# Fewer preparing steps, earlier hash products and later loads in batch one of a hash-attention and SwiGLU kernel

## The chip, the cores and the metric

The kernel runs on one core of one Trainium2 chip. The metric is device time in microseconds (us), measured on the chip; every run's output was compared with the reference and was correct unless said otherwise. A run counts as fast when it is within 1.5% of the fastest of its kernel.

## The reference, cut to what matters

```python
def _attn_ref(q, k, v, proj):              # q, k, v: 4 x 8 x 768 x 64, proj: 64 x 6
    q_bits = (einsum('bhsd,dk->bhsk', q, proj) > 0)
    k_bits = (einsum('bhsd,dk->bhsk', k, proj) > 0)
    mask = q_bucket[:, :, :, None] == k_bucket[:, :, None, :]    # buckets from the 6 bits
    scores = np.where(mask, scale * q @ k.T, -1e9)
    attn = softmax(scores)
    return attn @ v
def _moe_ref(x, w_gate, w_val, w_out):     # x: 3072 x 512, d_ff 1536
    g = x @ w_gate
    return (g * sigmoid(g) * (x @ w_val)) @ w_out
```

The attention's output (4 batches of 768 rows, 8 heads of 64) is x, reshaped to 3072 x 512.

## The kernel before

Two heads make a pair; each batch has four pairs, and each pair is worked in two halves of 384 queries with six score units each. While batch one's attention runs there is no expert product to fill gaps with, so its halves follow each other on TensorE: six score units, then six attend products. The hash products of a pair (L403) are turned into signs by ScalarE, and a transfer on the SP queue (the sign transfer, L420) copies those of q to a second place, where the score products read them. In between, VectorE prepares the expert weights for later in small steps: three per weight piece (L302, L304, L307) and four for the block sums of a finished group (L336), after which GpSimd writes the blocks to DRAM and fetches the first ones back.

The main loop, cut:

```python
for u in range(0, N, NCH):                 # u: first score unit of a half, NCH = 6
    n, half, _ = units[u]
    gating = u >= LATE                     # true once batch one's attention is over
    for c in range(NCH):
        score(u + c)
        if u + c == 2 or not gating and half == 1 and c == NCH - 3:
            prepare_pair(1)                # hash products of the next pair
        if c == 1 and half == 0 and 0 < n <= NP:
            total(n - 1)                   # softmax sums of the pair before
        if c:
            add(u + c)                     # VectorE, L514 and L518
    if n <= NP:
        finish(waiting)                    # norm of the pair before, L551
        finish(rest)
    ...
    for c in range(NCH):
        attend(u + c)
    if half == 1:
        load(n + 2, "qkv" if gating else "v")
    elif not gating:
        prepare_pair(2 if u > 0 else 4)
        load(n + 2, "qk")
    finish(first)
    prepare_on(0 if u == LATE else 4)      # preparing steps
    ...
    prepare_on(0 if LATE - NCH <= u <= LATE else 3)
```

The softmax sums and their reciprocal. The sum uses the one `av` buffer of PSUM that the attend products use too, and the reciprocal is spread over the partitions by eight 48 KB transfers on the SP queue:

```python
def total(n):
    ps = av_ps.tile([P, 512], FP32, tag="av", name="sum") if b == 0 else bank("sum")
    for h in range(2):
        for half in range(2):              # L531
            nc.tensor.matmul(ps[g : g + BLOCK, 0:HQ], ones, t[half][:, h, :], ...)
    nc.vector.reciprocal(r, ps[:, 0:HQ])   # L539
    for half in range(2):
        for h in range(2):
            for at in (h * D, h * D + BLOCK):
                nc.sync.dma_start(t[at : at + BLOCK, half, :], r[g : g + BLOCK, :])   # L544
    waiting.append(lambda: norm(n, t))     # norm is L551, on VectorE
```

Of the kernel before, what the change touches and what calls it, by code (L numbers as in the profile page):

```python
# [18 lines left out]
def kernel(  # L19
# [16 lines left out]
    NCH = S // P  # L36
# [3 lines left out]
    NP = H // 2  # L40
# [36 lines left out]
    def fetch(n, name, queue, half=None):  # L77
        b, pr = pairs[n]
        if name == "v":
            t = raws["v", n] = raw.tile([P, 2, NCH, D], FP32, tag="vraw", name="vraw")  # L80
            queue.dma_start(
                t.rearrange("p h c d -> p h (c d)"),
                v[b, 2 * pr : 2 * pr + 2].rearrange("h (p c) d -> p h (c d)", c=NCH),
            )
            return
        src = q if name == "q" else k
        if not half:
            raws[name, n] = raw.tile([P, NCH, 2, D], FP32, tag=name + "raw", name=name + "raw",
                                     bufs=1)
        t = raws[name, n]  # L90
        if n <= NP:
            cs = slice(None) if half is None else slice(half * CH, (half + 1) * CH)
            for h in range(2):
                queue.dma_start(t[:, cs, h, :],
                                src[b, 2 * pr + h].rearrange("(p c) d -> p c d", c=NCH)[:, cs, :])
            return


        blocks = t.rearrange("p c a b -> p (c a b)").rearrange(
            "p (c a d) -> p c a d", a=P // BLOCK, d=BLOCK)  # L100
        for h in range(2):
            for x in range(D // BLOCK):
                at = h * D + x * BLOCK
                queue.dma_start(  # L104
                    blocks[at : at + BLOCK],
                    src[b, 2 * pr + h][:, x * BLOCK : (x + 1) * BLOCK].rearrange(
                        "(a p c) d -> p c a d", c=NCH, p=BLOCK))

    def load(n, names):
        if n < len(pairs):  # L110
            for name in names:
                fetch(n, name, nc.sync)
# [179 lines left out]
    def scale_ahead():  # L292
        scale_to(min(progress["piece"] + 4, progress["scaled"] + 1))
# [70 lines left out]
    def prepare_on(n):  # L364
        for _ in range(n):
            next(preparing, None)
# [102 lines left out]
    LATE = NP * 2 * NCH  # L469
# [5 lines left out]
    def score(u):  # L475
        n, half, c = units[u]
        qs = slice(half * HQ, (half + 1) * HQ)
        ks = slice(c * P, (c + 1) * P)
        sc = [bank("sc")[:, 0:HQ] for _ in range(2)]
        for x, start in ((T, True), (bits, False)):  # L480
            if u < 2 and not start:
                prepare_pair(1)
            for h in range(2):
                rows = slice(h * D, (h + 1) * D)
                nc.tensor.matmul(sc[h], x["k", n][rows, ks], x["q", n][rows, qs],  # L485
                                 start=start, stop=not start)
        for h in range(2):
            nc.scalar.activation(weights(u)[:, h, 0:HQ], sc[h], AF.Exp,  # L488
                                 scale=SCALE * (OFF / 2 if n <= NP else 1.0))
# [19 lines left out]
    def add(u):  # L509
        n, half, c = units[u]  # L510
        a = weights(u)
        if c == 1:
            acc[n, half] = att.tile([P, 2, HQ], FP32, tag="acc", name="acc")
            nc.vector.scalar_tensor_tensor(out=acc[n, half], in0=weights(u - 1)[:, :, 0:HQ],  # L514
                                           scalar=S * EPS / P, in1=a[:, :, 0:HQ],
                                           op0=ALU.add, op1=ALU.add)
        elif c > 1:
            nc.vector.tensor_tensor(acc[n, half], acc[n, half], a[:, :, 0:HQ], op=ALU.add)  # L518

    def total(n):  # L520



        b, pr = pairs[n]

        ps = av_ps.tile([P, 512], FP32, tag="av", name="sum") if b == 0 else bank("sum")
        t = [acc.pop((n, half)) for half in range(2)]
        for h in range(2):
            for half in range(2):
                g = (2 * h + half) * BLOCK  # L530
                nc.tensor.matmul(ps[g : g + BLOCK, 0:HQ], ones, t[half][:, h, :],  # L531
                                 start=True, stop=True)
        if b == 0:
            space = wo.rearrange("p f m -> p (f m)")
            space = space[:, n % 2 * 3 * HQ : (n % 2 + 1) * 3 * HQ].rearrange("p (x q) -> p x q", q=HQ)
            r, t = space[:, 2, :], space[:, 0:2, :]
        else:
            r, t = t[1][:, 0, :], t[0]
# [3 lines that stand above are left out]
                g = (2 * h + half) * BLOCK  # L542
                for at in (h * D, h * D + BLOCK):
                    nc.sync.dma_start(t[at : at + BLOCK, half, :], r[g : g + BLOCK, :])  # L544
        waiting.append(lambda: norm(n, t))
        if pr == NP - 1:
            push_ffn(b)
# [200 lines left out]
    def prepare_pair(count):  # L748
        for _ in range(count):
            rest.extend(f for f in steps.pop(0)() or [] if f)  # L750

    def finish(todo):
        while todo:
            todo.pop(0)()
# [5 lines left out]
    for u in range(0, N, NCH):  # L760
        n, half, _ = units[u]
        gating = u >= LATE
        if u == MOVE:
            progress["late"] = True
            for t in late_ring:
                nc.gpsimd.memset(t[:, :, HQ:AW], 1.0)
        for c in range(NCH):
            score(u + c)
            if u + c == 2 or not gating and half == 1 and c == NCH - 3:
                prepare_pair(1)  # L770
            if c == 1 and half == 0 and 0 < n <= NP:
                total(n - 1)
            if c:
                add(u + c)
        if n <= NP:
            finish(waiting)
            finish(rest)
        if not gating and half == 0:
            steps = front(n + 1)
        if not gating and half == 0 and u > 0:  # L780
            prepare_pair(2)
        for _ in range(1 if u else 2):
            scale_ahead()
        for c in range(NCH):
            attend(u + c)
        if not gating:
            scale_ahead()
        if half == 1:
            load(n + 2, "qkv" if gating else "v")
        elif not gating:  # L790
            prepare_pair(2 if u > 0 else 4)
            load(n + 2, "qk")
        finish(first)
        prepare_on(0 if u == LATE else 4)
        chores = []
        if half == 1 and n >= NP:
            total(n)
            if n + 1 < len(pairs):
                chores = [None] + steps.pop(0)()
        prepare_on(0 if LATE - NCH <= u <= LATE else 3)  # L800
        if not gating:
            continue
        if n + 1 < len(pairs) and half == 0:
            steps = front(n + 1)
            chores = [None, steps.pop(0), None, steps.pop(0)]

        credit += 14 if n < 2 * NP else 15.75
        end = True
        part = 0
        while atoms and (credit > 0 or not end):  # L810
            size, atom, end = atoms.pop(0)
            credit -= size
            atom()
            part += size
            if part >= 11 or u + NCH == N and part >= 6:
                finish(waiting)
                if u + NCH == N:
                    finish([first.pop(0) for _ in range(min(2, len(first)))])
            if 5 < part < 14 if u == LATE else part < 9:
                prepare_on(size)  # L820
            if 6 < part < 11 or u == LATE and part > 10:
                scale_ahead()
            for _ in range(size):
                if chores:
                    step = chores.pop(0)
                    chores.extend(step and step() or [])
        while chores:
            step = chores.pop(0)
            chores.extend(step and step() or [])
# [34 lines left out]
```

## Time and profile before

| | |
|---|---|
| median of the first 3 runs | 1002.44 us (1001.71 to 1003.04) |
| TensorE busy | 990.2 of 1000.3 us in the profiled run |
| first expert product (L575) | 113.72 us |
| waits of TensorE in batch one of 0.3 us and more | 1.67 and 1.38 (reciprocal), 0.35 (additions), 1.17 (signs) |

How to read the views: an instruction's row in order of time is start, duration, engine, source line, operation, what it writes and reads, how many were run together, and in brackets how long its engine had been idle before it and what ended that. SPq and POOL rows of DMA operations are issues; the time to landing is told apart. Two more rows of the kernel before will matter. The first is from VectorE in order of time, the second from the list of DMA issues (count, size of each, median us from issue to landing):

```profile
93.74 1.02 DVE L551 SCALAR_TENSOR_TENSOR xT<-xT,e,wo 128x768 f32<-128x768 f32 x1 [1.46 <-DMA wo<-wo]
```

```profile
wo<-wo SPq DMA_DIRECT2D x32, 48.0 KB, 2.7
```

VectorE waits 1.46 us for the spread reciprocal of the fourth pair's half before it can go on with its queue, and the 32 transfers that spread batch one's reciprocals take 2.7 us in the median.

### The profile page before, as it was taken

The numbers are of one execution on the slowest core, as the hardware profiler recorded it, in microseconds if no ns is written. First come the engines' busy times: TensorE is split into PE (matmuls) and PEld (weight loads), VectorE is DVE, ScalarE is ACT, GpSimd is POOL, SyncE is SP. The second block draws the span as 40 slices with busy tenths as digits, with TensorE's granted clock in tenths as the row PEclk, the third lists the DMA queues.
The fourth block names the chain that finished last, engine by engine and source line by source line (L and its number), as shares of the span: only waits on it lengthen the run. The fifth ranks groups of instructions, "written<-read, shape, count | busy, mean of one in ns | idle before, by whom it ended". The sixth has DMA issues, their size and how long they took to land.

```text
span 1000.3 us, 12465 instructions
## 1 busy us (share of the span) xinstructions
PE 990.2 (99%) x4597; PEld 599.8 (60%) x4597; DVE 570.7 (57%) x892; ACT 398.4 (40%) x885; POOL 101.5 (10%) x200
## 2 busy tenths in 40 slices
PE   9999999999999999999999999999999999999998
PEld 4444455555576765555557775555556786555687
DVE  5888998887873624556564443554556442435431
ACT  6988555465323214444342223334343211222200
POOL 3222022221000000000000000000000000111000
PEclk9999999999999999999999999999999999999999
DMA  7777595885213032333331204333122012323001
GB/s 230 214 252 244 146 259 161 216 291 148 76 43 76 22 96 84 87 100 95 97 103 34 69 17 116 92 90 100 44 84 77 22 38 64 105 82 111 29 27 37
DMA packets 120749, 106.95 MB, mean 107 GB/s; under 512 B 89264, under 2 KB 104080, under 8 KB 120688
## 3 DMA queue, kind: packets, MB, share of 16 engines
q0 software_dynamic: 19104, 73.28, 22.9%
q1 hardware_dynamic: 100784, 32.67, 14.3%
q8 instruction: 36, 0.59, 0.3%
q10 hardware_dynamic: 800, 0.20, 0.1%
q14 instruction: 25, 0.20, 0.1%
HBM read 81.79 MB, written 17.30 MB: 99 GB/s over the span
## 4 chain that ended last, share of the span: by engine, by line
PE 87%; DMA 2%; DVE 1%; SPq 1%; ACT 1%; issue 1%; POOL 0%; DVEq 0%; POOLq 0%
PE up L575 43%; PE po L575 22%; PE sc L485 12%; PE av L500 9%; PE sum L531 1%; DMA words<-in_moe_w_out_dram 1%; PE hps L403 1%; SPq L104 1%; DMA wo<-wo 1%; DMA qb<-qb 0%; DMA room<-ram 0%; DVE room L359 0%; ACT A L488 0%; DVE wo L539 0%; DVE acc L518 0%
## 5 line engine op out<-in xcount | busy, mean ns | idle before, releaser
L575 PE MATMUL up<-xT,room 128*128 128x384 f32 x768 | 260.9, 488 | 0.0
L575 PEld LDWEIGHTS up<-xT,room 128*128 128x128 f32 x768 | 144.6, 190 | 106.7 <-issue 9.8
L575 PE MATMUL up<-xc,room 128*128 128x384 f32 x576 | 197.4, 486 | 0.0
L485 PE MATMUL sc<-qT,kT 64*128 64x384 f32 x768 | 161.5, 494 | 0.2 <-DVE c L562 0.2
L575 PEld LDWEIGHTS up<-xc,room 128*128 128x128 f32 x576 | 109.5, 190 | 76.3
L579 DVE TENSOR_TENSOR c<-c,up 128x384 f32<-128x384 f32 x72 | 39.8, 553 | 180.1 <-PE up L575 179.7
L518 DVE TENSOR_TENSOR acc<-acc,A 128x768 f32<-128x768 f32 x128 | 122.7, 958 | 14.4 <-ACT A L488 1.0
L318 POOL DMA_DIRECT2D room<-ram x96 | 52.4, 546 | 714.3 <-PE up L575 707.2
L488 ACT ACTIVATE A<-sc 128x384 f32<-128x384 f32 x256 | 105.6, 499 | 3.5 <-PE sc L485 3.4
L485 PEld LDWEIGHTS sc<-qT,kT 64*128 64x128 f32 x768 | 67.8, 186 | 55.5 <-issue 45.7
L710 ACT COPY o<-po 128x256 f32<-128x256 f32 x48 | 17.9, 372 | 200.5 <-PE po L575 200.5
L561 ACT ACTIVATE th<-c 128x384 f32<-128x384 f32 x72 | 37.6, 522 | 128.7 <-DVE c L562 89.2
L500 PE MATMUL av<-A,vraw 128*64 128x384 f32 (+1 forms) x512 | 88.2, 486 | 0.0
L579 DVE TENSOR_TENSOR o<-o,po 128x256 f32<-128x256 f32 x36 | 15.2, 421 | 111.6 <-PE po L575 82.5
L485 PE MATMUL sc<-qb,kb 64*128 64x384 bf16 x384 | 65.4, 323 | 1.7 <-DMA qb<-qb 1.2
L488 ACT ACTIVATE room<-sc 128x384 f32<-128x384 f32 x128 | 54.0, 495 | 32.6 <-PE sc L485 32.6
L575 PE MATMUL po<-wo,hid 128*128 128x256 f32 x288 | 66.9, 382 | 0.0
L575 PE MATMUL po<-wo,room 128*128 128x256 f32 x288 | 66.3, 379 | 0.1
L575 PE MATMUL po<-room,hid 128*128 128x256 f32 x288 | 66.1, 379 | 0.0
L500 PEld LDWEIGHTS av<-A,vraw 128*64 128x64 f32 x512 | 36.7, 137 | 46.0 <-issue 44.1
L638 ACT COPY c<-up 128x384 f32<-128x384 f32 x72 | 34.4, 478 | 69.1 <-PE up L575 69.1
L575 PEld LDWEIGHTS po<-wo,hid 128*128 128x128 f32 x288 | 54.1, 190 | 12.1 <-issue 4.9
(110 smaller groups left out, 969.4 us busy)
## 6 DMA issues: line engine op xcount, KB each, us to landing
room<-ram POOLq DMA_DIRECT2D x48, 512.0 KB, 4.8
room<-ram POOLq DMA_DIRECT2D x48, 384.0 KB, 3.9
vraw<-in_v_dram SPq DMA_DIRECT2D x16, 384.0 KB, 3.3
ram<-room POOLq DMA_DIRECT2D x12, 512.0 KB, 4.8
out_dram<-o SPq DMA_DIRECT2D x48, 128.0 KB, 1.7
room<-in_moe_w_out_dram POOLq DMA_DIRECT2D x10, 512.0 KB, 6.3
qraw<-in_q_dram SPq DMA_DIRECT2D x48, 96.0 KB, 3.2
hid<-in_moe_w_gate_dram POOLq DMA_DIRECT2D x9, 512.0 KB, 6.9
```

The lines of the kernel that those rows point to most:

```text
L104: queue.dma_start(blocks[at : at + BLOCK], src[b, 2 * pr + h][:, x * BLOCK : (x + 1) * BLOCK].rearrange("(a p c) d -> p c a d", c=NCH, p=B ...
L318: nc.gpsimd.dma_start(places[k % 2][:, PARTS[go], :], ram[k % NG][:, PARTS[go], :])
L403: nc.tensor.matmul(tile_[i * BLOCK : (i + 1) * BLOCK, 0:HQ], hash_w, T[name, n][:, half * HQ : (half + 1) * HQ], start=True, stop=True)
L485: nc.tensor.matmul(sc[h], x["k", n][rows, ks], x["q", n][rows, qs], start=start, stop=not start)
L488: nc.scalar.activation(weights(u)[:, h, 0:HQ], sc[h], AF.Exp, scale=SCALE * (OFF / 2 if n <= NP else 1.0))
L500: nc.tensor.matmul(ps[h * D : (h + 1) * D, 0:width], raws["v", n][:, h, c, :], a[:, h, 0:width], start=c == 0, stop=c == NCH - 1)
L518: nc.vector.tensor_tensor(acc[n, half], acc[n, half], a[:, :, 0:HQ], op=ALU.add)
L561: nc.scalar.activation(th, g, AF.Tanh, scale=0.5)
L575: nc.tensor.matmul(ps, a, x, start=start and i == 0, stop=i == len(pairs_) - 1, skip_group_check=True)
L579: nc.vector.tensor_tensor(o, a, b, op=op)
L638: nc.scalar.copy(tile_of(g, spot), c)
L710: nc.scalar.copy(o, c)
```

## The change

The intent is to take the three kinds of stall in batch one away. (A) VectorE has two preparing steps fewer after each second half of batch one, so that additions and reciprocal come earlier; the steps are caught up in batch two. (B) The hash products come one score unit earlier in second halves. (C) The sixth pair's q and k loads move from the fourth pair's first half to the end of its second half, behind the transfer of signs that waited for them on the SP queue.

```diff
-            if u + c == 2 or not gating and half == 1 and c == NCH - 3:
+            if u + c == 2 or not gating and half == 1 and c == 2:
                 prepare_pair(1)
...
         if half == 1:
-            load(n + 2, "qkv" if gating else "v")
+            load(n + 2, "qkv" if n + 2 > NP else "v")
         elif not gating:
             prepare_pair(2 if u > 0 else 4)
-            load(n + 2, "qk")
+            if n + 2 <= NP:
+                load(n + 2, "qk")
...
-        prepare_on(0 if LATE - NCH <= u <= LATE else 3)
+        prepare_on(0 if LATE - NCH <= u <= LATE else 3 if gating or not half else 1)
...
-            if 5 < part < 14 if u == LATE else part < 9:
+            if 5 < part < 14 if u == LATE else part < (9 if u < LATE + 3 * NCH else 11):
                 prepare_on(size)
```

## The prediction

> **What bounds the kernel now.** I read the page's first part first, then busy time by stretch, then the order-of-time lists of TensorE, VectorE and the SP queue, and last the chain of waits.
>
> ```profile
> PE 990.2 (99%) x4597; PEld 599.8 (60%) x4597; DVE 570.7 (57%) x892; ACT 398.4 (40%) x885; POOL 101.5 (10%) x200
> ```
>
> TensorE is busy for 99% of the span, and the change neither adds nor removes a matmul. So only TensorE's stalls can be won, and they are few. Busy time by stretch, cut at the borders of the score-and-attend halves of batch one, shows where:
>
> ```profile
> 43.41:53.45 10.04, 10.04 (x69) 4.42 (x68) 7.45 (x11) 9.91 (x22) 2.43 (x5) 1.00 0.60 156
> 53.45:67.63 14.18, 12.46 (x82) 5.83 (x80) 13.32 (x16) 10.25 (x25) 4.80 (x8) 1.00 0.94 344
> 67.63:77.68 10.05, 10.05 (x69) 4.42 (x68) 7.42 (x12) 9.92 (x22) 0.58 (x1) 1.00 0.58 154
> 77.68:92.12 14.44, 12.65 (x83) 5.84 (x81) 13.68 (x16) 10.34 (x25) 3.71 (x7) 1.00 0.85 292
> ```
>
> The columns are: stretch, its length, then busy time of PE, PEld, DVE, ACT and POOL. Second halves (10.04, 10.05) have no stall. A first half adds a sum (0.78) and two sets of transposes (0.80 each), so some 11.45 us would do. The third and fourth pairs' first halves take 14.18 and 14.44: 2.7 and 3.0 us lost, with DVE busy for 94% of them. TensorE in order of time names the stalls:
>
> ```profile
> 60.25 0.87 PE L387 MATMUL tps<-ident,kraw 128*128 128x128 f32 x6
> 62.79 1.52 PE L500 MATMUL av<-room,vraw 128*64 128x386 f32 x8 [1.67 <-DVE wo L539]
> ...
> 87.27 1.52 PE L500 MATMUL av<-room,vraw 128*64 128x386 f32 x8 [1.38 <-DVE wo L539]
> ...
> 104.41 0.32 PE L485 MATMUL sc<-qb,kb 64*128 64x384 bf16 x1 [1.17 <-DMA qb<-qb]
> ```
>
> The attend product waits for the reciprocal (L539) because both use the one av buffer of PSUM. A stretched sum adds to it (the sum at 55.39 took 1.49 where 0.85 is usual). VectorE just before that reciprocal:
>
> ```profile
> 55.90 0.69 DVE L307 CUSTOM_DVE_ANT_0 room<-hid,room 128x1024 uint16<-128x1024 uint16 x1
> 56.50 0.42 DVE L302 TENSOR_SCALAR room<-room 128x512 int32<-128x512 int32 x1
> 56.96 0.69 DVE L304 SCALAR_TENSOR_TENSOR room<-hid,room 128x512 int32<-128x512 int32 x1
> 57.68 0.69 DVE L307 CUSTOM_DVE_ANT_0 room<-hid,room 128x1024 uint16<-128x1024 uint16 x1
> 58.29 0.42 DVE L302 TENSOR_SCALAR room<-room 128x512 int32<-128x512 int32 x1
> 58.75 0.69 DVE L304 SCALAR_TENSOR_TENSOR room<-hid,room 128x512 int32<-128x512 int32 x1
> 59.57 0.69 DVE L307 CUSTOM_DVE_ANT_0 room<-hid,room 128x1024 uint16<-128x1024 uint16 x1
> 60.18 2.55 DVE L539 RECIPROCAL wo<-sum 128x384 f32<-128x384 f32 x1
> ```
>
> Seven preparing steps of the expert weights, 4.3 us, stand between the last addition and the reciprocal. The third stall, at 104.41, is the SP queue's: the sign transfer's wait for the queue.
>
> ```profile
> 92.46 2.75 SPq L104 DMA_DIRECT2D qraw<-in_q_dram  x4
> 95.25 3.83 SPq L104 DMA_DIRECT2D kraw<-in_k_dram  x4
> 99.59 0.55 SPq L420 DMA_DIRECT2D qb<-qb  x1
> ```
>
> The signs were ready on ScalarE at 97.9; the transfer was issued at 99.59 behind eight loads, and landed 4.8 us later.
>
> **What the Trainium skill says.** "PSUM — Partial Sum Buffer", section "Engine vs sequencer instructions": the queues of ScalarE, VectorE and GpSimdE are strict FIFO. The trace agrees: the reciprocal at 60.18 starts when the seventh step is over, though its sum was complete at 56.8. "DMA: Bandwidth & Descriptors", section "Anatomy of one DMA": a transfer has a fixed part of about 2 us, mostly the receipt of the last byte. The sign transfer's median of 1.9 us agrees; the one of 4.8 was among the loads. "Perfetto Trace Analysis", section "Identifying Performance Opportunities" (Optimization Strategy), says to find the gaps of the engine in question and what it waits for; that is the method here.
>
> **The change part by part.**
>
> 1. *Two steps fewer.* The order of instructions shows, between the last addition of a second half and the next reciprocal, 5 steps instead of 7 in front of the second, third and fourth pairs (4 of the fifth pair in both). All 144 steps remain; the missing 6 are made up by 2 more in each of three later halves (batch two's fourth to sixth). I walked VectorE by durations (L302 0.34 to 0.46, L304 0.72, L307 0.61, L336 0.67, reciprocal 2.46 to its successor, the five accumulations 5.05, L551 0.93).
>  - Second pair: the two L336 leave (1.34), the reciprocal is earlier, but TensorE never waited there.
>  - Third pair: the additions of the half before end at 54.95 instead of 55.9, so the sum isn't stretched (0.65); five steps (3.0) and the reciprocal end at 60.45. TensorE's transposes end at 60.75, so the stall goes: attend at 60.75 instead of 62.79, **2.0 us won**.
>  - Fourth pair: reciprocal end 60.45, plus 7.4 until the spread reciprocal is back (as in the trace), L551, seven steps (4.4), five accumulations: 78.15. Five steps (2.8) and the reciprocal: 83.45. Attend at 83.5 instead of 87.27, **3.8 won in all**.
>  - Fifth pair: 83.45 plus 6.6, L551, 4.3 of steps, 5.05: 100.3; L307 and three L336 (2.65) and the reciprocal: 105.4. Attend at 105.45 instead of 109.68: **4.2 in all**. VectorE is then the limit, and TensorE waits about 0.9 again. L551 behind it costs the first expert products about 0.2, so **4.0** is left.
> 2. *Loads behind the sign transfer.* That stall (1.2) goes, but it lies within the 4.2 above: without part 1's earlier additions the next limit is VectorE anyway. The loads move to about 94 us; their reader is VectorE's transpose at 120 (now some 116), so they hide.
> 3. *Hash products one unit earlier.* TensorE's and ScalarE's work is the same. The signs of q come 0.8 us earlier, useful only for the transfer. But the product's PSUM buffer (seven in turn) comes round one score unit earlier, at the first unit of the next half, and is read by the last sign of k, which ended 0.1 to 0.25 us after that unit's start (31.71 against 31.50; 53.56 against 53.45). That costs 0.1 to 0.3 in two places; the first is counted above (attend 0.16 later in the second pair), the second too.
> 4. *The bill in batch two.* The catching-up steps end where the expert products already stall: 1.07, 0.92 and 0.4 us at the starts of the halves at 216.8, 245.2 and 274.9. The chain of waits shows the first:
>
> ```profile
> 208.16 0.45 POOL room L318
> 208.61 0.07 issue
> 208.68 7.47 DMA words<-in_moe_w_out_dram
> 216.15 0.02 issue
> 216.18 0.67 ACT wo L288
> ```
>
>  A load of a weight piece stands behind a fetch of blocks in GpSimd's queue; ScalarE stops for it, then the gating, then a PSUM buffer. In the changed order another piece takes that place: it also has to wait for the copies of the last block, about 6 us later than now, so I put it 0 to 1 us later. In the second half the last waiting load stands behind the second fetch instead of the first (1.3 us): 0 to 1 later. In the third, two more L359 (0.6 each) fall into VectorE's unbroken run before 279: 0.3 to 1.2. I take 0.5, 0.5 and 0.7: **1.7 us lost**.
>
> Sum: 4.0 less 1.7 is 2.3 us; 1002.44 less 2.3 is about 1000.1.
>
> **The rivals.**
> - *The new bound is VectorE throughout batch one, so the gain is smaller.* For: its chain from reciprocal to reciprocal (23 us then 22) is as long as TensorE's work there, and the SP queue's eight spreads took 5.0 to 5.9 us. With 7.4 instead of 6.6 at the two later places it loses 1.6: a time of 1001.7. Against: the two later ones did take 6.5.
> - *The late stalls grow more.* For: pieces are two later all through the first expert halves, and loads took up to 9.4 us there. At 2 us for each of the first two, all is paid back: 1002 to 1003. Against: the catching up is done before the weights' last use, and the pieces in question are loaded at much the same places.
> - *Late stalls vanish, since fewer steps crowd them.* Then all 4 us stay: 998.4. For: three of the four waiting loads come earlier in that half. Against: the fourth does not.
> - *The hash move stalls more than said, or ScalarE becomes the limit* (it is busy 9.9 of 10.05 in second halves). Up to 0.3 at each of four places: 1001.
>
> **Range and chances.** The gain in batch one is 3 to 4.3, the loss later 0 to 3.5; with the spread of the runs before (1001.71 to 1003.04) I say 1000.1, and 998.4 to 1002.0 for 8 in 10. All visible stalls add to some 10 us, half of what 2% asks for (20 us), so faster by 2% can't come from this; slower by 2% would need a stall seen nowhere here. Chances: 0.005, 0.99, 0.005.
>
> **What would show it right or wrong.** Right: the wait for L539 before attends gone in the third pair, under 0.7 in the fourth, about 1 in the fifth; no wait for the sign transfer; a first score unit of a second or third pair held by 0.1 to 0.3; the first expert product near 109.5 instead of 113.7; late stalls at the three halves of 1 to 2 us each. Wrong: that product later than 111 (VectorE or the spreads bound it), or less than 1 us of the lead left after 330 us (the late stalls grew), or 4 us of it (they didn't).

## More of the kernel before

What a preparing step can set off on GpSimd's queue:

```python
def form(n):
    ...                                    # two block writes from the stage (L328, L330)
    for o, x, y, op in (...):
        nc.vector.tensor_tensor(o, x, y, op=op)      # L336
        yield True
    for pair, i in enumerate(group):
        nc.gpsimd.dma_start(ram[i][:, S2 : S4 + 1, :], formed[:, pair, :, :])   # L339
        if i < 2:
            for go in range(2):
                bring(i, go)               # L318: fetch of a block back from DRAM
# narrow(i) ends with load_words(i): L273, loads of the next weight pieces, 512 KB each
```

## The result and the profile after

The changed kernel takes **1007.97 us** in the median of 4 runs (1006.93 to 1008.95); the kernel before took 1002.08 (1000.92 to 1003.04) in its 4 runs. The ratio is **1.0059** (95% interval 1.0042 to 1.0077). Ratios here are the mean time of one kernel's fast runs over that of the other's fast runs of the same rounds, so they are not quite the ratio of the medians. The time is 7.9 us above the predicted 1000.1 and outside the predicted range. The change made the kernel about 6 us slower. All outputs are right.

The same part of the page, and busy time by stretch of the kernel after (stretch, length, busy PE, PEld, DVE, ACT, POOL, granted clock with 1.00 for full speed, DMA share, GB/s), cut at the third, fourth and fifth pairs' first halves:

```profile
PE 994.0 (99%) x4597; PEld 601.1 (60%) x4597; DVE 570.1 (57%) x892; ACT 399.9 (40%) x885; POOL 101.2 (10%) x200
```

```profile
53.95:67.13 13.18, 12.44 (x80) 5.64 (x78) 12.45 (x14) 10.19 (x24) 3.42 (x7) 1.00 0.91 317
77.20:91.16 13.96, 12.60 (x84) 5.85 (x82) 13.16 (x15) 10.14 (x24) 3.23 (x6) 1.00 0.61 190
101.18:137.17 35.99, 31.40 (x126) 15.86 (x125) 32.21 (x49) 16.42 (x35) 7.61 (x13) 0.91 0.61 157
```

The fifth pair's first half, which includes the first expert products, in the kernel before:

```profile
102.20:132.01 29.81, 28.64 (x128) 15.02 (x126) 27.18 (x42) 16.47 (x36) 3.53 (x7) 1.00 0.60 159
```

The first stretch is cut 0.19 us late: the third pair's first score product stands at 53.76. From first score product to first score product that half got 0.80 us shorter (14.18 to 13.38) and the fourth's 0.50 (14.44 to 13.94). The fifth's got 6.18 us longer: idle time of TensorE grew from 1.17 to 4.59 us (3.42 more), and its busy time from 28.64 to 31.40 (2.76 more) for the same work, at a mean granted clock of 0.91. TensorE in order of time shows both:

```profile
62.30 1.52 PE L500 MATMUL av<-room,vraw 128*64 128x386 f32 x8 [0.24 <-DVE wo L539]
...
81.09 0.85 PE L531 MATMUL sum<-acc,ones 128*32 128x384 f32 x6 [1.25 <-DVE acc L518]
...
86.29 1.52 PE L500 MATMUL av<-room,vraw 128*64 128x386 f32 x8
...
108.42 1.50 PE L531 MATMUL sum<-acc,ones 128*32 128x384 f32 x6 [4.59 <-DVE acc L518]
109.85 1.65 PE L485 MATMUL sc<-qT,kT 64*128 64x384 f32 x4
...
118.91 8.01 PE L575 MATMUL up<-xT,room 128*128 128x384 f32 x24
```

The waits for the reciprocal (L539) are nearly gone, and so is the wait for the signs, as intended. In their place TensorE waits 4.59 us for the additions (L518) of the fourth pair, before the sum at 108.42. After that wait a group of four score products takes 1.65 us where 0.92 is usual; between 107 and 113 us the granted clock is 0.50. The attends of the third and fourth pairs come 0.5 and 1.0 us earlier than before; the first expert product comes 5.2 us later (118.91 against 113.72).

Why the additions are late is on VectorE, in order of time:

```profile
83.68 2.55 DVE L539 RECIPROCAL wo<-sum 128x384 f32<-128x384 f32 x1
...
87.15 4.15 DVE L518 TENSOR_TENSOR acc<-acc,A 128x768 f32<-128x768 f32 x4
98.05 1.02 DVE L551 SCALAR_TENSOR_TENSOR xT<-xT,e,wo 128x768 f32<-128x768 f32 x1 [6.75 <-DMA wo<-wo]
...
103.16 0.95 DVE L514 SCALAR_TENSOR_TENSOR acc<-room 128x768 f32<-128x768 f32 x1
```

The reciprocal starts 1.0 us earlier than before (83.68 against 84.67). But L551, which needs the spread, stands next in the queue and waits **6.75 us** instead of 1.46. All behind it waits too: seven preparing steps and the additions of the second half, which begin at 103.16 instead of 99.11.

The spread took so long because of what ran beside it. Issues of GpSimd in order of time, the kernel before first, then the kernel after:

```profile
78.26 1.09 POOL L318 DMA_DIRECT2D room<-ram  x2 [3.55 <-issue]
...
79.87 0.53 POOL L273 DMA_DIRECT2D words<-in_moe_w_val_dram  x1
80.39 0.53 POOL L273 DMA_DIRECT2D hid<-in_moe_w_val_dram  x1
```

```profile
85.40 1.09 POOL L318 DMA_DIRECT2D room<-ram  x2 [2.89 <-issue]
86.48 0.54 POOL L339 DMA_DIRECT2D ram<-room  x1
87.01 0.53 POOL L273 DMA_DIRECT2D words<-in_moe_w_val_dram  x1
87.53 0.53 POOL L273 DMA_DIRECT2D hid<-in_moe_w_val_dram  x1
```

The eight issues of the spread on the SP queue, before and after:

```profile
87.24 5.04 SPq L544 DMA_DIRECT2D wo<-wo  x8
```

```profile
86.26 6.32 SPq L544 DMA_DIRECT2D wo<-wo  x8
```

On GpSimd's queue it is the same burst of about 2.4 MB by the sizes in the list of DMA issues: two fetches of blocks (512 and 384 KB), a write of blocks and two loads of weight pieces (512 KB each). It follows the last L336 step. That step ended at about 73.8 us in the kernel before and at about 81.6 in the kernel after, since two fewer steps in each second half pushed it from one pair's half into the next. The spread was issued from 87.24 in the kernel before, 7 us after the burst (only two single loads, issued at 83.17 and 84.96, came in between), and from 86.26 in the kernel after, in the middle of it. The eight transfers landed within 1.9 to 5.1 us (median 3.6) before and 5.1 to 7.5 (median 6.4) after, and issuing them took 1.28 us longer. The list of DMA issues shows it over all four spreads of batch one, against 2.7 before:

```profile
wo<-wo SPq DMA_DIRECT2D x32, 48.0 KB, 5.1
```

### The profile page after: what moved, and what is told of

The parts are those of the page before. It is cut to its first block, busy times and chain, and to the rows that moved or that the text cites. A ratio compares the mean times of both kernels' runs of the same rounds, so it can differ in the third digit from the quotient of the medians.

```text
span 1006.9 us, 12470 instructions
## 1 busy us (share of the span) xinstructions
PE 994.0 (99%) x4597; PEld 601.1 (60%) x4597; DVE 570.1 (57%) x892; ACT 399.9 (40%) x885; POOL 101.2 (10%) x200
## 4 chain that ended last, share of the span: by engine, by line
PE 73%; issue 2%; DVE 1%; DMA 1%; ACT 0%; POOL 0%; POOLq 0%; DVEq 0%
PE up L575 34%; PE po L575 21%; PE sc L485 9%; PE av L500 7%; PE sum L531 1%; DMA room<-in_moe_w_out_dram 1%; PE hps L403 1%; DVE room L359 0%; DVE acc L518 0%; ACT A L488 0%; DVE wo L359 0%; DVE c L562 0%; POOL room L318 0%; ACT wo L288 0%; DVE hid L566 0%
## 5 line engine op out<-in xcount | busy, mean ns | idle before, releaser
L518 DVE TENSOR_TENSOR acc<-acc,A 128x768 f32<-128x768 f32 x128 | 122.7, 958 | 15.0 <-ACT A L488 2.2
```

The lines of the kernel that those rows point to most:

```text
L518: nc.vector.tensor_tensor(acc[n, half], acc[n, half], a[:, :, 0:HQ], op=ALU.add)
```

## The experiments

My theory: the fault is the order of VectorE's queue. L551 waits there for transfers ahead of the additions, and the moved steps carried GpSimd's burst into those transfers. Rivals: the loads of part C do the harm; the hash move does; VectorE has simply too much work before its additions and reciprocals. Ten kernels were run; the changed kernel itself is an eleventh. Each ratio is against the kernel before in the same rounds, whose medians were 1001.69, 1002.28 and 1002.17 us in the three sets (first to fourth; fifth to eighth; last two).

### Each part alone

Part A alone (both changes of `prepare_on`):

```diff
-        prepare_on(0 if LATE - NCH <= u <= LATE else 3)
+        prepare_on(0 if LATE - NCH <= u <= LATE else 3 if gating or not half else 1)
-            if 5 < part < 14 if u == LATE else part < 9:
+            if 5 < part < 14 if u == LATE else part < (9 if u < LATE + 3 * NCH else 11):
```

> Only the two preparing steps fewer and their catching up. Theory (the steps moved GpSimd's transfers of block sums and weight pieces into the spread of the fourth pair's reciprocal, VectorE waits in order for that spread, the additions and then the sum are late): the wait before L551 at the fourth pair is over 5 us, the sum of the fifth pair's first half waits over 3 us, time 1005 to 1009. Rival (the hash products' new place, or the loads of q and k moved to 96 us, is what costs): time at most 1002, no such wait.

Measured: 1006.42 us in 6 runs (1005.73 to 1009.07), ratio 1.0047 (1.0030 to 1.0063). Most of the slowdown is here. L551 of the fourth pair waits 6.02 us, and the spread lands in 4.9 to 7.9 us. (As what ended that wait the profile names a load of q, which follows the spread on the SP queue.) The wait of the sum that the theory expected did not come: the sign transfer stops TensorE first, and the clock then falls to 0.50 for some three microseconds.

```profile
104.77 0.32 PE L485 MATMUL sc<-qb,kb 64*128 64x384 bf16 x1 [3.16 <-DMA qb<-qb]
```

Part B alone (hash products at the third score unit):

```diff
-            if u + c == 2 or not gating and half == 1 and c == NCH - 3:
+            if u + c == 2 or not gating and half == 1 and c == 2:
```

> Only the hash products behind the third score unit. Theory: within 1 us of before, 1001 to 1003, L551's wait at the fourth pair stays near 1.5 us. Rival (this part costs): 1005 or more.

Measured: 1001.97 us in 6 runs (1000.48 to 1002.46), ratio 0.9997 (0.9981 to 1.0014). The wait for the signs shrinks from 1.17 to 0.64 us, and the first expert product comes at 111.9 instead of 113.7, but nothing of it is to be seen in the median; the profiled run was the fastest of the six. The predicted stall of 0.1 to 0.3 us is not to be seen either. Part B is not the cause.

Part C alone:

```diff
-            load(n + 2, "qkv" if gating else "v")
+            load(n + 2, "qkv" if n + 2 > NP else "v")
-            load(n + 2, "qk")
+            if n + 2 <= NP:
+                load(n + 2, "qk")
```

> Only the loads of q and k behind the transfer of signs. Theory: the 1.2 us wait for the sign transfer is gone, but the reciprocal on VectorE ends at the same time, so at most 0.5 us of it is won: 1001 to 1002.5. Rival (this part costs): 1005 or more.

Measured: 1004.82 us in 6 runs (1002.49 to 1007.55), ratio 1.0028 (1.0009 to 1.0047): a miss. The wait for the signs is gone, but the moved loads hold the SP queue where the fifth pair's reciprocal is to be spread. Here is the SP queue in this run, then TensorE:

```profile
103.03 6.09 SPq L104 DMA_DIRECT2D kraw<-in_k_dram  x4
...
110.16 6.31 SPq L544 DMA_DIRECT2D wo<-wo  x8
```

```profile
118.94 4.78 PE L575 MATMUL up<-xT,room 128*128 128x384 f32 x14 [2.07 <-DVE xT L551]
```

Issuing four loads took 6.09 us, where the eight took 6.58 together in the kernel before. The spread behind them is issued late and takes 6.31 us to issue instead of the usual 5; L551 waits 3.52 us and TensorE 2.07 at the second set of expert products. The loads of q ahead of them (from 98.64) were issued while GpSimd issued writes of blocks (96.49 to 100.56), so the slow issue may not be the loads' alone. Part C moves a wait from the signs to the fifth pair's spread.

### The wait moved out of the way

The changed kernel, but in second halves only is the norm (L551) put after the additions, so VectorE no longer stands before them:

```diff
         if n <= NP:
-            finish(waiting)
+            if half == 1 or n == NP:
+                finish(waiting)
             finish(rest)
```

> All of the change, and in batch one the normalising of a pair (L551, which waits for the spread reciprocal) stands behind the additions of the second half instead of behind those of the first. No transfer is taken away. Theory (VectorE waiting in order is the carrier): the sum of the fifth pair's first half waits under 1 us, time 1000 to 1003, some 5 to 7 us under the changed kernel. Rival (the transfers slow something else, or ScalarE or TensorE is the limit): 1006 or more.

Measured: **997.07 us** in 6 runs (996.51 to 997.98), ratio 0.9950 (0.9935 to 0.9964), some 11 us below the changed kernel and under the expected 1000 to 1003. It is the strongest evidence: steps, burst and loads are as in the changed kernel, and only the place of the waiting instruction differs. The fourth pair's spread was still slow (3.6 to 8.2 us to landing, median 5.8), but harmless. VectorE and TensorE in order of time:

```profile
89.75 0.96 DVE L514 SCALAR_TENSOR_TENSOR acc<-room 128x768 f32<-128x768 f32 x1
...
95.50 1.01 DVE L551 SCALAR_TENSOR_TENSOR xT<-xT,e,wo 128x768 f32<-128x768 f32 x1
```

```profile
102.94 1.52 PE L500 MATMUL av<-room,vraw 128*64 128x386 f32 x8
104.29 2.76 PE L500 MATMUL av<-A,vraw 128*64 128x386 f32 x16
106.98 5.43 PE L575 MATMUL up<-xT,room 128*128 128x384 f32 x16
```

The additions begin at 89.75 instead of 103.16, L551 does not wait, and the rows have no bracket: TensorE did not wait. The first expert product comes at 106.98, even earlier than predicted for the change (109.5).

### The burst moved out of the way, and put in the way

The changed kernel with the fetch of block 1 delayed until batch one's attention is over; the rest of the burst, which no longer stands behind it, is then issued by 84.2 us, before the spread at 85.9:

```diff
-            if i < 2:
+            if i == 0:
                 for go in range(2):
                     bring(i, go)
...
         gating = u >= LATE
+        if u == LATE:
+            for go in range(2):
+                bring(1, go)
```

> All of the change, but the fetch of block 1 (0.9 MB, at 85.4 us in the changed kernel) is asked for only at the start of the fifth pair, and what stood behind it in GpSimd's queue comes some 3 us earlier. Theory (the burst of GpSimd's transfers slows the spread of the fourth pair's reciprocal): L551's wait there falls from 6.75 us to under 4.5, time 1002 to 1006. Rival (the spread is slow for another reason, such as its own queue): wait over 6 us, 1007 or more.

Measured: 1004.12 us in 4 runs (1003.95 to 1007.80), ratio 1.0017 (0.9987 to 1.0048). The spread lands in 1.9 to 4.7 us again and L551 waits 1.40 instead of 6.75 us:

```profile
92.38 1.02 DVE L551 SCALAR_TENSOR_TENSOR xT<-xT,e,wo 128x768 f32<-128x768 f32 x1 [1.40 <-DMA wo<-wo]
```

The first expert product is at 111.9. The other waits are untouched: TensorE waits 1.26 us for the additions at 57.25, 0.85 at the fifth pair's attend, and 1.45 at the second set of expert products for the spread behind part C's loads. So the burst makes the 6.75 us, but it is not all that the change costs.

The kernel before with a burst of its own: five unused copies of 512 KB inside DRAM, issued by GpSimd just ahead of the fourth pair's spread:

```diff
                 total(n - 1)
+                if n == 3:
+                    for i in range(5):
+                        junk = dram.tile([P, 2 * PIECE], I32, tag=f"junk{i}", name="junk")
+                        nc.gpsimd.dma_start(junk[:, :], moe_w_gate[...])
```

> The kernel before with five more transfers of 512 KB on GpSimd's queue, DRAM to DRAM, unused, issued at about 85.5 us, just ahead of the spread of the fourth pair's reciprocal; nothing else. Theory: the spread lands 3 to 6 us later, L551 waits over 4.5 us, the sum of the fifth pair waits, time 1004 to 1009. Rival (such a burst is harmless to the small transfers): L551's wait stays under 2.5 us, 1001 to 1003.

Measured: 1011.91 us in 4 runs (1011.12 to 1013.03), ratio 1.0087 (1.0060 to 1.0113), above the expected 1004 to 1009. VectorE in order of time:

```profile
97.39 1.02 DVE L551 SCALAR_TENSOR_TENSOR xT<-xT,e,wo 128x768 f32<-128x768 f32 x1 [5.57 <-DMA wo<-wo]
```

The copies alone, without any moved step, make L551 wait 5.57 us; the spread lands in 5.3 to 6.3 us. They slow the loads on the SP queue too, so that the signs come 9.58 us late for TensorE at 112.37. The time therefore shows more than the one cost; the wait of L551 is the reading that counts. The copies both read and write DRAM, so they stand in for the burst and do not repeat it.

### Fewer steps taken away

The whole change, but with two steps fewer only in the third pair's second half:

```diff
-        prepare_on(0 if LATE - NCH <= u <= LATE else 3 if gating or not half else 1)
+        prepare_on(0 if LATE - NCH <= u <= LATE else 1 if u == 5 * NCH else 3)
```

> All of the change, but the two steps fewer only in the third pair's second half, so that the second block's sums and the fetch stay at their place of before (76 to 82 us). Theory: L551 at the fourth pair waits under 3 us, no long wait of the fifth pair's sum; the loads still hold up the last spread as in the run with the loads alone, so 1000 to 1004. Rival (fewer steps are bad in themselves): 1006 or more.

Measured: 1009.91 us in 4 runs (1008.93 to 1011.67), ratio 1.0068 (1.0040 to 1.0096): a miss. Batch one went as expected: L551 of the fourth pair waits 1.46 us, and the first expert product is at 112.1. But batch two has a stall that no other kernel has. ScalarE in order of time, then TensorE:

```profile
190.65 0.66 ACT L288 ACTIVATE wo<-room 128x512 f32<-128x512 f32 x1 [6.00 <-DMA room<-in_moe_w_out_dram]
```

```profile
193.95 1.01 PE L485 MATMUL sc<-qT,kT 64*128 64x384 f32 x1 [4.74 <-DVE c L562]
```

The load of that piece was issued at 180.66, behind two fetches of blocks which waited 4.51 us for TensorE, and took 9.97 us to land; in the kernel before the last load there was issued at 175.39, ahead of the fetches at 179.42. ScalarE waits for it, and the gating behind it, and TensorE 4.74 us, with the clock at 0.50 afterwards: from the start of that half (186.69 against 188.07) to that of the next (223.02 against 216.82) a lead of 1.38 us turned into a lag of 6.20. A moved step thus moved a load to the other side of a fetch, which is the kind of late cost that the prediction's part 4 reckons with, at several times its size. That it is this load is read from the trace, not tested.

### Is the change needed at all?

The kernel before with only the later norm:

```diff
-            finish(waiting)
+            if half == 1 or n == NP:
+                finish(waiting)
```

> The kernel before with L551 behind the additions of the second half, and nothing of the change. Theory (VectorE's in-order wait for the spread is the main cost of batch one, in the kernel before too): the waits for L539 at the third and fourth pairs shrink to under 1 us, 996 to 1000. Rival (the two steps are what counts, as the change has it): at least 1001.

Measured: 1004.33 us in 4 runs (1002.06 to 1005.46), ratio 1.0009 (0.9974 to 1.0043): a miss. The waits for the reciprocal are gone (attends at 60.40 and 82.32), but TensorE arrives sooner at the sign transfer. That was issued only at 97.71, behind eight loads that took from 87.61 to 97.2 to issue, and TensorE waits 4.91 us for it; the clock is 0.50 until 109:

```profile
103.19 0.48 PE L485 MATMUL sc<-qb,kb 64*128 64x384 bf16 x1 [4.91 <-DMA qb<-qb]
```

So part C is needed once VectorE is out of the way.

The kernel before with the later norm and part C, and no step moved:

```diff
-            finish(waiting)
+            if half == 1 or n == NP:
+                finish(waiting)
...
-            load(n + 2, "qkv" if gating else "v")
+            load(n + 2, "qkv" if n + 2 > NP else "v")
...
-            load(n + 2, "qk")
+            if n + 2 <= NP:
+                load(n + 2, "qk")
```

> The kernel before with two edits only: the normalising products (L551) of a pair stand behind the second half's additions, and the sixth pair's q and k loads behind the sign transfer; no preparing step is moved. Theory (VectorE's queue was stopped by its wait for the spread, and the sign transfer by the loads; the moved steps themselves are not needed): batch one without a wait of TensorE over 0.5 us, first expert product near 107, as in the changed kernel with that one move (106.98), and no late bill of moved steps, so about 1.4 us under it: 995 to 997, ratio 0.993 to 0.995. Rival (the moved steps are needed, as VectorE still comes late with its seven steps ahead of a reciprocal): waits for the reciprocal of 1 us and more at the attends of the third and fourth pairs, 998 to 1001.

Measured: 998.83 us in 5 runs (997.60 to 999.52), ratio 0.9963 (0.9950 to 0.9977). There is no wait for a reciprocal in the third and fourth pairs (attends at 60.15 and 82.10), so the moved steps are not needed for those. Two waits are left, 0.91 us for the signs at 98.98 and the one behind part C's loads:

```profile
112.69 4.78 PE L575 MATMUL up<-xT,room 128*128 128x384 f32 x14 [0.90 <-DVE xT L551]
```

The time lies in the rival's range, so the expectation missed by 1.8 us; the waits that the rival named are not there, though, and the two that are left add up to 1.81 us. The best kernel (997.07 us), with steps and hash products moved as well, has neither of them, but its ratio of 0.9950 (0.9935 to 0.9964) is not clear of this one's. The lead in the first expert product over the kernel before is 5.4 us, and 4.4 are left at the last one (935.4 against 939.8); the loss is the 0.90. In the best kernel, with the moved steps, the lead is 6.7 and 5.2 are left (934.6): 1.5 us lost, of which a wait of 1.20 for the gating at 241.87 is the largest part that the trace shows. I take that for the late bill of the moved steps; it was not tested.

The same with part B added:

```diff
-            if u + c == 2 or not gating and half == 1 and c == NCH - 3:
+            if u + c == 2 or not gating and half == 1 and c == 2:
```

> The run before plus the hash products one score unit earlier. Theory (the hash move is worth nothing by itself, as its own run showed 0.9997): within 0.5 us of the kernel without it. Rival (it costs a stall of 0.1 to 0.3 us at the first score unit of the next half, as predicted, at two to four places): 0.3 to 1 us longer. Other rival: it makes the sign transfer earlier by some 0.8 us, 0 to 0.8 us shorter.

Measured: 998.92 us in 6 runs (997.77 to 1000.00), ratio 0.9969 (0.9955 to 0.9983), the same as without B. The wait for the signs (0.91) is gone and the first expert product comes 1.0 us earlier, at 107.3; in turn the one behind the loads grows from 0.90 to 2.00. The best kernel differs from this one by the moved steps alone. It has no wait behind the loads, and its ratio is 0.9950 (0.9935 to 0.9964); as the intervals overlap, a gain from the moved steps is likely there but not shown.

## Why the prediction was wrong

**Where it failed.** The step that failed is in part 1, the fifth pair: "83.45 plus 6.6, L551, 4.3 of steps, 5.05: 100.3". Here 83.45 is the end of the reciprocal. It ended at 86.15, already 2.7 us late, because the spreads of the pairs before had been late too (below). And the spread reciprocal was back 11.9 us after that end (L551 ran from 98.05), not 6.6: another 5.3 us. The term was carried over from the trace of the kernel before, as if a transfer's time belonged to the transfer; yet the same steps that were moved carry GpSimd's burst with them. In the run with fewer steps in the third pair only, where that burst stayed 4 us ahead of the spread, the spread was back after 6.6 us (85.96 to 92.56), as the prediction had it. With both delays the additions end at 108.28 instead of 100.3. The slow clock after the wait then adds 2.76 us, which no term of the sum foresaw. The first expert product was predicted at 109.5 and came at 118.91.

**Third pair, 2.0 us won.** The attend came at 62.30, 0.5 us earlier than before, 0.8 if one allows for a start that was 0.27 us later in the profiled run. The reciprocal's wait did go, but for 0.24 us, as predicted. But the sum was still split by a wait of 0.44 us for the additions, because L551 of the second pair waited 3.82 us instead of 2.37:

```profile
46.21 1.02 DVE L551 SCALAR_TENSOR_TENSOR xT<-xT,e,wo 128x768 f32<-128x768 f32 x1 [3.82 <-DMA wo<-wo]
```

It is the same wrong term, only smaller: 9.0 us from the end of the reciprocal to L551, against 7.5 in the kernel before. So the additions ended at 56.84, not at 54.95.

**Fourth pair, 3.8 us won in all.** The attend came at 86.29: 1.0 us won. The sum waited 1.25 us for the additions, since L551 of the third pair waited 3.15 us instead of 2.25; its spread was back after 8.3 us, not 7.4. The walk had the right order; each spread was too short.

**A sum.** "Some 11.45 us" for a first half doesn't follow from its parts: 10.05 and 0.78 and twice 0.80, less the 0.78 of hash products that a first half lacks, make 11.65. In the best kernel the third and fourth pairs' halves took 11.82 and 11.68, so 2.4 and 2.8 us were to be won there, not 2.7 and 3.0. The walk doesn't use the figure.

**The signs.** Right that the stall goes. But the prediction said that the loads "hide"; it looked only for their reader, at 116 us, and not at the next user of the SP queue. By itself, part C cost 0.3% (0.9 to 4.7 us by its interval).

**The hash move.** A stall of 0.1 to 0.3 us was predicted and none was seen; worth nothing in its own run.

**The late bill, 1.7 us.** Right in size: from the first expert product to the last, the lag grew from 5.2 to 6.5 us, so 1.3 us. It fell otherwise than predicted (0.5, 0.5 and 0.7): by the starts of the halves, 0.1 us was won in the first of the three, and 0.8 and 0.7 lost in the others; which waits made that was not traced. One more kernel showed that a moved step can cost a wait of 4.74 us at once.

**The rivals.** The first, that VectorE becomes the bound with 7.4 instead of 6.6 at the spreads, named the right place, but with the size again taken from the old trace; the measured one was 11.9. The prediction's own test, "that product later than 111", did show it wrong.

**What stays open.** That a burst delays the spread is shown in both directions. Whether this happens in the 16 shared DMA engines, at DRAM or in the issuing is not separated. The three parts alone cost 4.7, 3.1 and nothing to speak of, which is more than the 5.9 us of all together, though with intervals of up to 2 us to either side not clearly so; that they overlap is argued from the traces, and was not tested pair by pair.

## What to carry to other kernels

Put an instruction that waits for a transfer behind the work on its engine that others wait for; the best kernel here is 0.5% faster than the kernel before, though the same change without that one line is 0.6% slower. When a step is moved, follow all that it sets off, and look at what those transfers will run beside: a time from issue to landing belongs to a moment, not to an instruction. A wait of TensorE of some 3 us or more may be paid for twice, as its clock falls and takes microseconds to return (here after waits of 3.16 us and more, and not after one of 2.07).

## What the Trainium skill lacked or had wrong

- "DMA: Bandwidth & Descriptors", section "Anatomy of one DMA": its fixed cost of roughly 2 us is given for GpSimd's path, while the spread goes over the SP queue. There 1.9 us was the least that a 48 KB transfer took in most spreads; beside GpSimd's transfers of 512 KB it was 5.1 to 7.5. The page gives no figure for a small transfer beside large ones.
- The same page, section "Issuing engines are not separate DMA queues": it calls the time to initiate a DMA "usually small relative to the DMA itself". For one transfer of the spread that holds (0.59 us in the median to issue, 3.6 to landing), but not for a row of them on one queue: eight spreads took 5.04 us to issue, and four loads of k took 6.09. The part that says transfers of all engines share 16 DMA engines and interleave fits all the runs here, though none separates it from other causes.
- "TensorE: Matmul & The Clock Gate", section "What's actually happening": that the clock falls to half after an idle window of about 3.4 us agrees roughly with the trace. It was granted 0.50 after waits of 3.16 to 9.58 us, the shortest of them less than that window, and 1.00 after one of 2.07. Coming back took 4.7 us of work after the wait of 4.59, and about 5.8 after the wait of 4.91, more than one busy window of 3.4 us; as the page lets the window run freely, up to two of them (6.8 us, an estimate from its figure) need not contradict it.
- "PSUM — Partial Sum Buffer", section "Engine vs sequencer instructions", has the strict order of VectorE's queue. No page has a figure for what it costs to put an instruction that waits for a transfer early in such a queue. Here that was 1007.97 us against 997.07.
